# Hedgehog linear attention and a maxout FFN on one core: transposes by the crossbar, 64-row paired projections, strips of nine tiles, and an order written by hand

## The chip, the cores and the metric

The kernel runs on one core of a Trainium2 chip. A core has five engines that each work through an instruction queue of their own: TensorE (PE in the profile, with its weight loads shown apart as PEld), VectorE (DVE), ScalarE (ACT), GpSimd (POOL) and SyncE (SP), which here only issues transfers. Sixteen DMA engines move data. PE writes only to the accumulator memory PSUM, which has eight banks of 512 fp32 values in each of 128 partitions. The metric is the device time of one execution in microseconds (us), lower is better.

## The reference

```python
q, k, v: (8, 8, 576, 64) fp32          # batch, heads, tokens, head width
w_phi: (64, 128)   moe_w1, w2, w3: (512, 768)   moe_w_out: (768, 512)

def phi(x):                            # 64 -> 256 features
    proj = x @ w_phi                                        # (..., 576, 128)
    proj = proj - max(abs(proj), axis=-1, keepdims=True)
    return concatenate([exp(proj), exp(-proj)], axis=-1)
q_p, k_p = phi(q), phi(k)
kv  = einsum('bhsf,bhsd->bhfd', k_p, v)
z   = sum(k_p, axis=2)
num = einsum('bhsf,bhfd->bhsd', q_p, kv)
den = einsum('bhsf,bhf->bhs', q_p, z)[..., None] + 1e-6
x   = (num / den), heads side by side  # (4608, 512)
h   = maximum(maximum(x @ w1, x @ w2), x @ w3)
out = h @ w_out                        # (4608, 512) fp32
```

## The kernel before

**Units.** The 64 pairs of batch and head are taken four at a time: 16 units of four heads, 2,304 rows of q, k and v each, so two units make one batch of 576 tokens. A unit's rows lie in 18 tiles of 128 rows (two heads of 576 rows fill nine tiles, half a tile each: partitions 0 to 63 hold the first head, 64 to 127 the second). That block of two heads is called a strip.

**Loads.** `loads` brings q, k and v of a unit as fp32 by three queues (q by SP L214, k by ACT L216, v by POOL L218), one unit ahead, into double buffers. `prepare` then has DVE cast q and k side by side into `qk_bf` (L226, L227) and v into `v_bf` (L228). PE transposes the 18 tiles of `qk_bf` (L234, `tps`) and DVE copies them from PSUM to `qkT` (L235), with q's 64 rows in partitions 0 to 63 and k's in 64 to 127.

**Groups.** `group` takes four tiles (five groups a unit, the last of two tiles). Per tile a 64-row matmul gives the projection of q (`psq`, L265) and one that of k (`psk`, L267), rows on the partitions. DVE takes both maxima (L269 `mq_bf`, L271 `mk_f`), ACT makes exp of plus and minus the keys' projection (L273, L274). Then the same q projection is computed a second time with the features on the partitions (`psTt`, L278, one matmul of 512 columns on 128 rows, half of them zero weights), q's maxima are subtracted from it by one matmul per tile (L281, weights `mq_bf` spread over 128 columns, times minus the identity), and ACT makes both exponentials `Eq1T`, `Eq2T` (L298, L299). The keys' maxima are not subtracted; `emit_va_vb` scales v with exp of them instead (ACT L252, L253, POOL L254, L256).

**Two units later** (`LAG`): `kv_strip` sums keys times values over the nine tiles of a strip by 64-row matmuls of 65 columns (`kvps`, L316), `xt_nums` multiplies with the queries' features (`psnd`, L333, L335), DVE divides (`rden`, `x_sb`, L338 to L343), and `xt_trans` transposes the result on PE (`pxT`, L356) and copies it to `xT_all` on DVE (L360).

**FFN.** Chunks of up to 512 tokens are cut into items: for each of six blocks of 128 hidden features twelve matmuls of 512 columns (`ups`, L137), one copy on ACT and two maxima on DVE (L147 to L152); then per 128 tokens six matmuls (`ops`, L161), a copy on ACT (L169) and a store by POOL's queue (L112). `ffn_filler` puts one item behind a group or a transposed head.

**PSUM.** One pool, `psA`, with eight buffers of one bank serves every tile that PE writes. The order of each engine's instructions comes from a scheduler that goes by the order of the code and by which buffers are free.

Of the kernel before, what the change touches and what calls it, by code (L numbers as in the profile page):

```python
# [12 lines left out]
LN = mybir.ActivationFunctionType.Ln  # L14
ALU = mybir.AluOpType
# [4 lines left out]
NTOK = B * S  # L20
# [3 lines left out]

UNITS = 16
UROWS = 2304
HU = 4
UT = UROWS // P
GROUPS = [(0, 4), (4, 4), (8, 4), (12, 4), (16, 2)]
HALVES = [(0, 5), (5, 4)]  # L30
LAG = 2
# [3 lines left out]
def kernel(  # L35
    ctx: ExitStack,
    tc: tile.TileContext,
    q: bass.AP,
    k: bass.AP,
    v: bass.AP,  # L40
    w_phi: bass.AP,
    moe_w1: bass.AP,
    moe_w2: bass.AP,
    moe_w3: bass.AP,
    moe_w_out: bass.AP,
    out: bass.AP,
):
    nc = tc.nc

    try:  # L50
        from concourse.hw_specs import get_activation_tables
        _tables = list(get_activation_tables(nc.m.arch).keys())
        _set_id = _tables.index("natural_log_exp_and_others")
    except Exception:
        _set_id = 6
    nc.scalar.add_instruction(
        mybir.InstLoadActFuncSet(
            act_func_set_id=_set_id,
            name=nc.get_next_instruction_name(),
            ins=[],  # L60
            outs=[],
# [3 lines left out]
    q_flat = q.rearrange("b h s d -> (b h s) d")  # L65
    k_flat = k.rearrange("b h s d -> (b h s) d")
    v_flat = v.rearrange("b h s d -> (b h s) d")

    const = ctx.enter_context(tc.tile_pool(name="const", bufs=1))
# [3 lines left out]
    negident = const.tile([P, P], BF16, name="negident")  # L73
    nc.gpsimd.tensor_single_scalar(negident, ident, -1.0, ALU.mult)
    wphi2 = const.tile([P, DF], BF16, name="wphi2")
    wphi_q = const.tile([P, DF], BF16, name="wphi_q")
    nc.gpsimd.memset(wphi_q[D:2 * D, :], 0.0)
    wphi_f = const.tile([P, DF], FP32, name="wphi_f")
    nc.sync.dma_start(wphi_f[0:D, :], w_phi)
    nc.sync.dma_start(wphi_f[D:2 * D, :], w_phi)  # L80
    nc.vector.tensor_copy(wphi2, wphi_f)
    nc.vector.tensor_copy(wphi_q[0:D, :], wphi_f[0:D, :])

    w_bf = [const.tile([P, DM // P, DFF], BF16, name=f"w{wi}_bf") for wi in range(3)]
    wout_bf = const.tile([P, DFF // P, DM], BF16, name="wout_bf")

    def load_weights():
        for wi, w_ap in enumerate((moe_w1, moe_w2, moe_w3)):
            nc.gpsimd.dma_start(w_bf[wi], w_ap.rearrange("(ct p) n -> p ct n", p=P))
        nc.gpsimd.dma_start(wout_bf, moe_w_out.rearrange("(ct p) n -> p ct n", p=P))  # L90

    raw = ctx.enter_context(tc.tile_pool(name="raw", bufs=2))
    vpool = ctx.enter_context(tc.tile_pool(name="vpool", bufs=2))
    qkp = ctx.enter_context(tc.tile_pool(name="qkp", bufs=2))
    epool = ctx.enter_context(tc.tile_pool(name="epool", bufs=3))
    mpool = ctx.enter_context(tc.tile_pool(name="mpool", bufs=2))
    kvpool = ctx.enter_context(tc.tile_pool(name="kvpool", bufs=3))
    denp = ctx.enter_context(tc.tile_pool(name="denp", bufs=2))
    ffp = ctx.enter_context(tc.tile_pool(name="ffp", bufs=2))
    psA = ctx.enter_context(tc.tile_pool(name="psA", bufs=8, space=bass.MemoryType.PSUM))  # L100

    xT_all = const.tile([P, DM // P, NTOK], BF16, name="xT_all")

    ffn_items = deque()
    ffn_pending = deque()
    out_dma_pending = deque()
    ffn_count = [0]

    def flush_out_dmas(keep: int = 0):
        while len(out_dma_pending) > keep:  # L110
            dram_ap, osb = out_dma_pending.popleft()
            nc.gpsimd.dma_start(dram_ap, osb)  # L112

    def flush_pending_ffn():
        while ffn_pending:
            ffn_items.append(ffn_pending.popleft())
            ffn_count[0] += len(ffn_items[-1])

    def pop_ffn_item():
        while ffn_items and not ffn_items[0]:  # L120
            ffn_items.popleft()
        if not ffn_items:
            return None
        item = ffn_items[0].popleft()
        ffn_count[0] -= 1
        return item

    def make_ffn_items(tok0: int, ntok: int):
        hT = ffp.tile([P, DFF // P, 512], BF16, name="hT", tag="hT")
        chunk_items = deque()  # L130

        for j in range(DFF // P):
            def item(j=j, hT=hT):
                def umat(i):
                    up = psA.tile([P, 512], FP32, name="ups", tag="b")
                    for ct in range(DM // P):
                        nc.tensor.matmul(  # L137
                            up[:, 0:ntok],
                            lhsT=w_bf[i][:, ct, j * P:(j + 1) * P],
                            rhs=xT_all[:, ct, tok0:tok0 + ntok],  # L140
                            start=(ct == 0),
                            stop=(ct == DM // P - 1),
                        )
                    return up
                u1 = umat(0)
                t1 = ffp.tile([P, 512], BF16, name="t1", tag="t1")
                nc.scalar.copy(t1[:, 0:ntok], u1[:, 0:ntok])  # L147
                u2 = umat(1)
                t2 = ffp.tile([P, 512], BF16, name="t2", tag="t2")
                nc.vector.tensor_tensor(t2[:, 0:ntok], t1[:, 0:ntok], u2[:, 0:ntok], ALU.max)  # L150
                u3 = umat(2)
                nc.vector.tensor_tensor(hT[:, j, 0:ntok], t2[:, 0:ntok], u3[:, 0:ntok], ALU.max)  # L152
            chunk_items.append(item)

        ntt = (ntok + P - 1) // P
        for tt in range(ntt):
            def item(tt=tt, hT=hT):
                mrow = min(P, ntok - tt * P)
                ops_ = psA.tile([P, DM], FP32, name="ops", tag="b")
                for j in range(DFF // P):  # L160
                    nc.tensor.matmul(  # L161
                        ops_[0:mrow, :],
                        lhsT=hT[:, j, tt * P:tt * P + mrow],
                        rhs=wout_bf[:, j, :],
                        start=(j == 0),
                        stop=(j == DFF // P - 1),
                    )
                osb = ffp.tile([P, DM], FP32, name="osb", tag="osb")
                nc.scalar.copy(osb[0:mrow, :], ops_[0:mrow, :])  # L169
                out_dma_pending.append((out[tok0 + tt * P:tok0 + tt * P + mrow, :], osb[0:mrow, :]))  # L170
            chunk_items.append(item)
        ffn_pending.append(chunk_items)

    def ffn_filler(n=1):
        for _ in range(n):
            item = pop_ffn_item()
            if item is None:
                return
            flush_out_dmas(keep=2)
            item()  # L180

    chunks = []
    tok = 0
    last_batch_start = (B - 1) * S
    while tok < NTOK:
        n = min(512, NTOK - tok)
        if tok < last_batch_start < tok + n:
            n = last_batch_start - tok
        chunks.append((tok, n))
        tok += n  # L190
    next_chunk = [0]

    def ffn_ready(tokens_done: int, final: bool = False):
        while next_chunk[0] < len(chunks):
            tok0, ntok = chunks[next_chunk[0]]
            if tok0 + ntok <= tokens_done:
                make_ffn_items(tok0, ntok)
                next_chunk[0] += 1
            else:
                break  # L200

    class Unit:
        def __init__(un, u):
            un.u = u
            un.b = u // 2
            un.hbase = (u % 2) * HU
            un.row0 = u * UROWS

        def loads(un):
            un.q_raw = raw.tile([P, UT, D], FP32, name="q_raw", tag="q_raw")  # L210
            un.k_raw = raw.tile([P, UT, D], FP32, name="k_raw", tag="k_raw")
            un.v_raw = raw.tile([P, UT, D], FP32, name="v_raw", tag="v_raw")
            r0 = un.row0
            nc.sync.dma_start(un.q_raw.rearrange("p (st j) d -> p st j d", st=2),  # L214
                              q_flat[r0:r0 + UROWS, :].rearrange("(st p j) d -> p st j d", st=2, p=P))
            nc.scalar.dma_start(un.k_raw.rearrange("p (st j) d -> p st j d", st=2),  # L216
                                k_flat[r0:r0 + UROWS, :].rearrange("(st p j) d -> p st j d", st=2, p=P))
# [41 lines left out]
        def group(un, gi):  # L259
# [43 lines left out]
            elif t0 + gsz == UT:  # L303
                un.emit_va_vb(9, UT)
# [147 lines left out]
```

## Time and profile before

| | |
|---|---|
| time, median of three runs | 447.31 us (445.69 to 449.65) |
| span of the profiled execution | 445.3 us |
| granted TensorE clock, mean | 0.951 |
| PE busy | 398.1 us (89%), 4,286 matmuls |
| DVE busy | 324.9 us (73%), 762 instructions |
| ACT busy | 207.8 us (47%), 514 |
| POOL busy | 116.7 us (26%), 145 |
| DMA moved | 41.62 MB, mean 93 GB/s |

The span runs from the first to the last instruction of the profiled execution; no other time of that execution was taken, and it lies 2.0 us below the median of the runs. Busy time of an engine is the union of its instructions' times; a matmul's time includes the run through the array, so that neighbours overlap, and how fast PE really works is read from the starts of one run of matmuls and the next. Instructions are named by tile and by line of the kernel.

### The profile page before, as it was taken

Reading aid. Unit: us, or ns where it says so; the run is one execution under the profiler, and the core shown is the slowest. Engines: PE = TensorE matmul, PEld = TensorE weight load, DVE = VectorE, ACT = ScalarE, POOL = GpSimd, SP = SyncE. Lnnn points to the kernel's source line nnn. Section 1 sums busy time; section 2 is a strip of 40 time slices with the busy share of each in tenths; the row PEclk is TensorE's granted clock in tenths of the full one; section 3 lists DMA queues with packets and bytes.
Section 4 is the critical chain, followed back from the end, with each engine's and each line's share of the span. In section 5 each row is a group of like instructions: output and inputs, shape, how many; then the busy total and the mean of one; then the engine's idle time right before and its main releaser. Section 6 shows DMA issues by size and latency. Waiting matters only on the chain.

```text
span 445.3 us, 10421 instructions
## 1 busy us (share of the span) xinstructions
PE 398.1 (89%) x4286; PEld 227.8 (51%) x4286; DVE 324.9 (73%) x762; ACT 207.8 (47%) x514; POOL 116.7 (26%) x145
## 2 busy tenths in 40 slices
PE   0599888998999899998999899989999989899993
PEld 0367566446564456455654556445644555444442
DVE  0697999975888689967897698868977876724331
ACT  1096746451754546562736275454656461132322
POOL 3156145023150504023422315050402240010101
PEclk9996796997999989998999899998999999999998
DMA  8999142512324033312531232001000100020202
GB/s 297 327 244 259 68 160 89 179 54 79 125 67 148 25 110 124 115 45 79 177 110 54 76 126 77 31 25 49 27 0 1 72 25 2 1 96 11 72 36 71
DMA packets 16479, 41.62 MB, mean 93 GB/s; under 512 B 1456, under 2 KB 3888, under 8 KB 16432
## 3 DMA queue, kind: packets, MB, share of 16 engines
q0 software_dynamic: 7568, 22.02, 16.9%
q10 hardware_dynamic: 4352, 9.44, 6.4%
q1 hardware_dynamic: 4512, 9.50, 6.3%
q8 instruction: 33, 0.54, 0.5%
q14 instruction: 14, 0.11, 0.1%
HBM read 34.67 MB, written 9.44 MB: 99 GB/s over the span
## 4 chain that ended last, share of the span: by engine, by line
PE 56%; issue 18%; ACT 9%; DVE 8%; DMA 4%; POOL 3%; SPq 0%; POOLq 0%; ACTq 0%
PE ups L137 22%; PE ops L161 7%; PE pxT L356 6%; PE psnd L333 4%; PE psq L265 4%; PE psTt L278 4%; PE tps L234 4%; PE psTt L281 3%; DMA q_raw<-in_q_dram 3%; ACT Eq1T L298 2%; ACT Eq2T L299 2%; PE psnd L335 2%; DVE mq_bf L269 2%; POOL va L254 2%; DVE qk_bf L227 2%
## 5 line engine op out<-in xcount | busy, mean ns | idle before, releaser
L137 PE MATMUL ups<-xT_all,w_bf 128*128 128x512 bf16 (+2 forms) x720 | 152.0, 358 | 0.1
L298 ACT ACTIVATE Eq1T<-psTt 128x512 bf16<-128x512 f32 (+1 forms) x96 | 51.5, 541 | 127.4 <-PE psTt L281 107.5
L137 PEld LDWEIGHTS <-w_bf 128*128 128x128 bf16 x720 | 62.3, 98 | 62.3 <-issue 0.6
L256 POOL TENSOR_TENSOR vb<-v_bf,em 128x585 bf16<-128x585 bf16 x32 | 37.6, 1176 | 147.2 <-ACT emn L253 86.7
L112 POOL DMA_DIRECT2D out_dram<-osb x37 | 22.7, 613 | 136.0 <-ACT osb L169 116.3
L161 PE MATMUL ops<-wout_bf,hT 128*128 128x512 bf16 (+1 forms) x222 | 56.1, 383 | 0.0
L299 ACT ACTIVATE Eq2T<-psTt 128x512 bf16<-128x512 f32 (+1 forms) x96 | 52.8, 551 | 0.0
L360 DVE COPY xT_all<-pxT 64x576 bf16<-64x576 bf16 x64 | 47.8, 746 | 6.2 <-PE pxT L356 5.5
L269 DVE TENSOR_REDUCE mq_bf<-psq 128x4 bf16<-128x512 f32 (+1 forms) x80 | 50.4, 630 | 2.5 <-PE psk L267 2.1
L271 DVE TENSOR_REDUCE mk_f<-psk 128x4 f32<-128x512 f32 (+1 forms) x80 | 50.1, 626 | 0.1
L333 PE MATMUL psnd<-kv_sb,Eq1T 128*128 128x65 bf16 (+1 forms) x320 | 38.3, 208 | 12.8 <-DVE kv_sb L322 11.3
L254 POOL TENSOR_TENSOR va<-v_bf,emn 128x585 bf16<-128x585 bf16 x32 | 38.5, 1204 | 5.6 <-ACT emn L253 5.6
L335 PE MATMUL psnd<-kv_sb,Eq2T 128*128 128x65 bf16 (+1 forms) x320 | 38.2, 205 | 0.0
L356 PE MATMUL pxT<-ident,x_sb 128*64 128x128 bf16 (+1 forms) x320 | 35.8, 225 | 2.4 <-DVE x_sb L341 2.3
L356 PEld LDWEIGHTS <-x_sb 128*64 128x64 bf16 (+1 forms) x320 | 23.0, 109 | 27.8 <-issue 17.9
L234 PE MATMUL tps<-ident,qk_bf 128*128 128x128 bf16 x288 | 26.1, 264 | 12.3 <-DVE qk_bf L227 12.3
L281 PE MATMUL psTt<-negident,mq_bf 128*128 128x128 bf16 x288 | 31.7, 232 | 5.0 <-DVE mq_bf L269 4.9
L265 PE MATMUL psq<-wphi_66,qkT 64*128 64x128 bf16 x288 | 32.7, 234 | 3.7 <-DVE qkT L235 3.7
L333 PEld LDWEIGHTS <-Eq1T 128*128 128x128 bf16 (+1 forms) x320 | 26.5, 105 | 17.8 <-DVE kv_sb L322 10.8
L267 PE MATMUL psk<-wphi_66,qkT 64*128 64x128 bf16 x288 | 32.3, 233 | 1.5 <-DVE xT_all L360 1.1
L278 PE MATMUL psTt<-qkT,wphi_q 128*128 128x512 bf16 (+1 forms) x80 | 32.0, 400 | 1.2 <-ACT Ek_969 L274 0.4
L281 PEld LDWEIGHTS <-mq_bf 128*128 128x128 bf16 x288 | 20.1, 102 | 22.8 <-DVE mq_bf L269 13.5
(309 smaller groups left out, 587.5 us busy)
## 6 DMA issues: line engine op xcount, KB each, us to landing
k_raw<-in_k_dram ACTq DMA_DIRECT2D x16, 576.0 KB, 4.7
v_raw<-in_v_dram POOLq DMA_DIRECT2D x16, 576.0 KB, 5.6
q_raw<-in_q_dram SPq DMA_DIRECT2D x16, 576.0 KB, 5.4
out_dram<-osb POOLq DMA_DIRECT2D x35, 256.0 KB, 2.5
w_bf<-in_moe_w_dram POOLq DMA_DIRECT2D x3, 768.0 KB, 12.4
wout_bf<-in_moe_w_out_dram POOLq DMA_DIRECT2D x1, 768.0 KB, 7.6
out_dram<-osb POOLq DMA_DIRECT2D x2, 128.0 KB, 2.3
wphi_f<-in_w_phi_dram SPq DMA_DIRECT2D x2, 32.0 KB, 4.9
```

The lines of the kernel that those rows point to most:

```text
L137: nc.tensor.matmul(up[:, 0:ntok], lhsT=w_bf[i][:, ct, j * P:(j + 1) * P], rhs=xT_all[:, ct, tok0:tok0 + ntok], start=(ct == 0), stop=(ct = ...
L161: nc.tensor.matmul(ops_[0:mrow, :], lhsT=hT[:, j, tt * P:tt * P + mrow], rhs=wout_bf[:, j, :], start=(j == 0), stop=(j == DFF // P - 1),)
L265: nc.tensor.matmul(psq[:, i, :], lhsT=un.qkT[0:D, cols], rhs=wphi2[0:D, :], start=True, stop=True)
L269: nc.vector.tensor_reduce(un.mq_bf[:, t0:t0 + gsz], psq[:, 0:gsz, :], AXX, ALU.max, apply_absolute_value=True)
L271: nc.vector.tensor_reduce(un.mk_f[:, t0:t0 + gsz], psk[:, 0:gsz, :], AXX, ALU.max, apply_absolute_value=True)
L278: nc.tensor.matmul(psTt[:, 0:ncols], lhsT=wphi_q, rhs=un.qkT[:, t0 * P:t0 * P + ncols], start=True, stop=False)
L281: nc.tensor.matmul(psTt[:, i * P:(i + 1) * P], lhsT=un.mq_bf[:, t0 + i:t0 + i + 1].to_broadcast([P, P]), rhs=negident, start=False, stop=( ...
L298: nc.scalar.activation(eq_view(un.Eq1T), src, EXP)
L299: nc.scalar.activation(eq_view(un.Eq2T), src, EXP, scale=-1.0)
L333: nc.tensor.matmul(psnd[0:ncolc, c, :], lhsT=un.Eq1T[:, col0:col0 + ncolc], rhs=kv_sb[:, 0, :], start=True, stop=False)
L356: nc.tensor.transpose(pxT[0:D, 128 * c:128 * c + ncolc], x_sb[0:ncolc, c, :], ident[0:ncolc, 0:ncolc])
L360: nc.vector.tensor_copy(dstv, srcv)
```

## The change

The kernel is written anew around the same mathematics; units, strips and the lag stay, and all of the following changes.

- **Loads and transposes.** POOL's queue loads k and q and casts them to bf16 on the way (`kn`, `qn`); SP's queue loads v as fp32. SP then issues two crossbar transposes per unit (`kT`, `qT`, 128x1152 each) in place of PE's 18 and DVE's copies. Loads are issued two units ahead with three buffers (four for v).
- **Projections.** A transposed block of 128 partitions holds two tiles, one in partitions 0 to 63, one in 64 to 127, so that two 64-row matmuls with weights `wphi` in both halves run as a pair, for k, for q, and for the second, transposed projection of q (`psT`). Steps are of three blocks, six tiles: three steps a unit, 48 in all.
- **q's maxima.** DVE writes them to a zeroed 128x128 tile `mq`, SP transposes it on the crossbar to `mT`, and six matmuls with constant weights `pick` subtract them two steps later.
- **Result.** `num_strip` treats both heads of a strip in one PSUM tile of two banks, DVE writes x of a batch to `x_main` (four groups of 128 tokens) and `x_rest` (the last 64), and SP transposes these on the crossbar (`xT`, `xrest`). The last ninth of the tokens of four batches is one FFN chunk of 256 tokens; every batch has one chunk of 512.
- **PSUM.** Two pools: `ps2`, two buffers of two banks, for `psk`, `psq`, `psT` and `nd` in turn; `ps1`, four buffers of one bank, for `kvps`, `ups` and `ops`.
- **Order.** The scheduler is off; the order is that of the code. `fill` puts FFN pieces (four or six matmuls each) at three places of a step, and `pace` spreads a batch's pieces over six steps, less a reserve of 5.0. Stores go by SP's queue.

```diff
+    ps2 = ctx.enter_context(tc.tile_pool(name="ps2", bufs=2, space=bass.MemoryType.PSUM))
+    ps1 = ctx.enter_context(tc.tile_pool(name="ps1", bufs=4, space=bass.MemoryType.PSUM))
+    ctx.enter_context(tc.manual_schedule())
...
+    def start_loads(u):
...
+        load(nc.gpsimd, un.kn, k_f, u)
+        load(nc.gpsimd, un.qn, q_f, u)
+        load(nc.sync, un.vn, v_f, u)
...
+    def transposes(un):
...
+        nc.sync.dma_start_transpose(un.kT, un.kn.rearrange("p s d -> p (s d)"))
+        nc.sync.dma_start_transpose(un.qT, un.qn.rearrange("p s d -> p (s d)"))
...
+    def project(dst, xT, b0):
+        for i in range(GB):
+            for e in range(2):
+                nc.tensor.matmul(dst[:, e, i * P:(i + 1) * P], lhsT=xT[e * D:(e + 1) * D, b0 + i, :],
+                                 rhs=wphi[e * D:(e + 1) * D, :], start=True, stop=True)
...
+    def queries(un, g):
...
+        nc.vector.tensor_reduce(mq[:, :, 0:GB], view(pq), AXX, ALU.max, apply_absolute_value=True)
+        mT = small.tile([P, P], BF16, name="mT", tag="mT", bufs=4)
+        nc.sync.dma_start_transpose(mT, mq.rearrange("p e d -> p (e d)"))
...
+    def transposed(un, g):
...
+        for e in range(2):
+            rows = slice(e * D, (e + 1) * D)
+            nc.tensor.matmul(pv[:, e], lhsT=wphi[rows, :],
+                             rhs=un.qT[rows, b0:b0 + GB, :].rearrange("d b (h p) -> d h b p", h=2),
+                             start=True, stop=False)
+        for i in range(GB):
+            for e in range(2):
+                rows = slice(e * D, (e + 1) * D)
+                nc.tensor.matmul(pv[:, e, :, i, :], lhsT=pick[rows, i, :],
+                                 rhs=mT[rows, :].rearrange("r (h p) -> r h p", h=2),
+                                 start=False, stop=(i == GB - 1))
+        for s in range(2):
+            nc.scalar.activation(un.Eq[s][:, :, :, b0 * D:(b0 + GB) * D],
+                                 pt[:, :, 0:GB * P].rearrange("f e (h n) -> f e h n", h=2),
+                                 EXP, scale=1.0 - 2.0 * s)
...
+    def finish_batch(b):
...
+        nc.sync.dma_start_transpose(xT, x_main.rearrange("p c n -> p (c n)"))
+        nc.sync.dma_start_transpose(xrest[:, :, b, :], x_rest)
...
+    for n in range(STEPS + 4):
+        u, g = divmod(n, NG)
...
+        us = pace(n)
+        tt = n - LAG_T
+        if 0 <= tt < STEPS:
+            transposed(units[tt // NG], tt % NG)
+        if n < STEPS:
+            pk = keys(units[u], g)
+        fill(us / 3)
+        if n < STEPS:
+            for s in range(2):
+                keys_exp(units[u], g, pk, s)
+            queries(units[u], g)
+            if g == 1 and u + 1 < UNITS:
+                transposes(units[u + 1])
+            if g == 2 and u + 2 < UNITS:
+                units[u + 2] = start_loads(u + 2)
+            if g >= 1:
+                scale_v(units[u], g - 1)
+        t = n - 3
+        if t >= 0:
+            r = t % NG
+            if r < 2 and t < STEPS:
+                kvs[t // NG, r] = kv_strip(units[t // NG], r)
+        fill(us / 3)
+        t = n - 4
+        if t >= 0 and t % NG < 2:
+            r = t % NG
+            num_strip(units[t // NG], r, kvs.pop((t // NG, r)))
+        fill(us / 3)
+        if t >= 0 and t % NG == 1:
+            done = units.pop(t // NG)
+            if done.half == 1:
+                enqueue(finish_batch(done.b))
+                if done.b % 4 == 3:
+                    enqueue(rest_chunk(done.b - 3))
+    fill(1e9)
```

What the change moves is seen best on three queues. First PE in the middle of the program, where a unit begins. Before, behind the last `psnd` of an older unit, with runs of equal rows cut to the first and the weight loads left out:

```order
L335 MATMUL psnd<-kv_sb,Eq2T 64x65
L234 MATMUL tps<-ident,qk_bf 128x128
L265 MATMUL psq<-wphi_66,qkT 128x128
L267 MATMUL psk<-wphi_66,qkT 128x128
L278 MATMUL psTt<-qkT,wphi_q 128x512
L356 MATMUL pxT<-ident,x_sb 64x128
L137 MATMUL ups<-xT_all,w_bf 128x512
L281 MATMUL psTt<-negident,mq_bf 128x128
```

And one step of the changed kernel on PE, with the engines that a row waits for:

```order
L189 MATMUL psT<-qT,wphi 128x384 [waits Activation_49]
L195 MATMUL psT<-mT,pick 128x2x64 [waits DMAHW5_49]
L152 MATMUL psk<-wphi,kT 128x128 [waits PE_49]
L289 MATMUL ups<-xT,w_bf 128x512
L152 MATMUL psq<-wphi,qT 128x128 [waits Activation_49]
L222 MATMUL kvps<-va_1432,Ek_1427 128x65 [waits Pool_49]
```

The transposes `tps` and `pxT` are gone, a piece of the FFN stands between the keys' and the queries' projections, and `psq` now waits for ACT, because its PSUM buffer is the one that the step's `psT` leaves. Second, SP's queue. Before, it only loads q, each load when DVE has read the buffer:

```order
L79 DMA wphi_f<-in_w_phi_dram 64x128
L214 DMA q_raw<-in_q_dram 128x2x576 x2
L214 DMA q_raw<-in_q_dram 128x2x576 [waits DMAHW2_49,DVE_49]
L214 DMA q_raw<-in_q_dram 128x2x576 [waits DMAHW4_49,DMAHW0_49,DVE_49]
L214 DMA q_raw<-in_q_dram 128x2x576 [waits DMAHW6_49,DVE_49]
```

In the changed kernel, around the end of one batch:

```order
L106 DMA_TRANSPOSE kT<-kn 128x9x128 [waits DMASW6_49]
L107 DMA_TRANSPOSE qT<-qn 128x9x128 [waits DMAHW3_49,DMASW7_49]
L179 DMA_TRANSPOSE mT<-mq_105 128x128 [waits DMAHW4_49,DVE_49]
L83 DMA vn<-in_v_dram 128x2x576 [waits DMAHW5_49,Pool_49]
L329 DMA out_dram<-osb 2x64x512 [waits DMAHW6_49,Activation_49]
L323 DMA_TRANSPOSE xT<-x_main 128x16x128 [waits DMAHW7_49,DVE_49]
L324 DMA_TRANSPOSE xrest<-x_rest 128x4x64 [waits DMAHW0_49,DVE_49]
L329 DMA out_dram<-osb 2x64x512 [waits DMAHW1_49,Activation_49]
L179 DMA_TRANSPOSE mT<-mq_106 128x128 [waits DMAHW2_49,DVE_49]
```

SP had 18 transfers and now has 152, and all crossbar transposes, loads of v and stores stand in one line; each waits for its data and for the transfer eight places ahead of it (DMAHW0 to DMAHW7 are the semaphores that they share in turn). Third, DVE over one step of the changed kernel:

```order
L165 TENSOR_REDUCE mk<-psk 128x2x3
L296 TENSOR_TENSOR t_1353<-t_1327,ups 128x512
L177 TENSOR_REDUCE mq_105<-psq 128x2x3
L299 TENSOR_TENSOR hT<-t_1353,ups 128x512
L250 RECIPROCAL rd<-nd 128x8
L251 RECIPROCAL rr<-nd 64x2
L252 TENSOR_TENSOR x_main<-nd,rd 128x2x4x64
L254 TENSOR_TENSOR x_rest<-nd,rr 64x128
```

Casts of the inputs, copies of `qkT` and copies to `xT_all` are gone from DVE; what is left are the reductions, now 48 of each kind over six tiles, the FFN's maxima, `kv_sb` and the division for two heads at once.

More of the change, by code (lines that the diff above doesn't have):

```diff
@@ L23, with hedgehog_ffn @@
 P = 128
[L25 to L26 removed]
 HU = 4
[L28 to L31, printed above, removed]
[L34 to L47 removed]
+UNITS = B * H // HU
+UROWS = HU * S
+NT = 18
+NB = 9
+NG = 3
+GB = 3
+J = 9
+TOK = (0, 1, 4, 5, 8)
+CT = DM // P
+FT = DFF // P
+D1 = D + 1
+STEPS = UNITS * NG
+LAG_T = 2
+RESERVE = 5.0
+@with_exitstack
+def hedgehog_ffn(ctx, tc, q, k, v, w_phi, moe_w1, moe_w2, moe_w3, moe_w_out, out):
     nc = tc.nc
@@ L71 @@
+    wphi = const.tile([P, DF], BF16, name="wphi")
+    nc.vector.tensor_copy(wphi, wphi_f)
+    NQ = 4
+    mqs = [const.tile([P, 2, D], BF16, name=f"mq{i}") for i in range(NQ)]
+    for t in mqs:
+        nc.gpsimd.memset(t, 0.0)
     ident = const.tile([P, P], BF16, name="ident")
     make_identity(nc, ident)
[L73 to L90, printed above, removed]
@@ L100 @@
[L100 to L148, printed above, removed]
-                t2 = ffp.tile([P, 512], BF16, name="t2", tag="t2")
[L150 to L172, printed above, removed]
@@ new lines, in kv_strip @@
+    def kv_strip(un, r):
+        kv = [ps1.tile([P, 2, D1], FP32, name="kvps", tag="b") for _ in range(2)]
+        for s in range(2):
+            Ek = tiles(un.Ek[s])
+            for j in range(J):
+                for h in range(2):
+                    rows = slice(h * D, (h + 1) * D)
+                    nc.tensor.matmul(kv[h][:, s, :], lhsT=Ek[rows, r * J + j, :],
+                                     rhs=un.va[s][rows, r * J + j, :], start=(j == 0), stop=(j == J - 1))
+        kv_sb = small.tile([P, 2, 2, D1], BF16, name="kv_sb", tag="kv_sb", bufs=4)
+        for h in range(2):
+            nc.vector.tensor_copy(kv_sb[:, h], kv[h])
+        return kv_sb
```

432 lines of the change are left out of this document (179 added, 253 removed).

## The prediction

> **What bounds the kernel now.** I read the page's busy times first, then its slices and its chain.
>
> ```profile
> PE 398.1 (89%) x4286; PEld 227.8 (51%) x4286; DVE 324.9 (73%) x762; ACT 207.8 (47%) x514; POOL 116.7 (26%) x145
> PE   0599888998999899998999899989999989899993
> PE 56%; issue 18%; ACT 9%; DVE 8%; DMA 4%; POOL 3%; SPq 0%; POOLq 0%; ACTq 0%
> ```
>
> PE is busy for 398.1 of 445.3 us, and the chain that ends last runs mostly on it; DVE is a good second. Since a matmul's record includes its run through the array, I ask next how many stretches PE is really full in.
>
> ```profile
> 10.00:40.00 30.00, 22.21 (x256) 15.05 (x256) 23.51 (x47) 18.16 (x50) 11.96 (x13) 0.94 1.06 263
> 220.00:250.00 30.00, 28.98 (x307) 15.62 (x306) 23.06 (x51) 15.85 (x41) 8.95 (x10) 1.00 0.25 80
> 400.00:430.00 30.00, 30.00 (x145) 13.91 (x143) 13.22 (x20) 7.87 (x14) 2.16 (x4) 1.00 0.09 31
> ```
>
> Columns are the stretch, its length, busy time of PE, PEld, DVE, ACT and POOL, granted clock, DMA share, GB/s. Before there is FFN work (10 to 40) PE has gaps of a quarter; in the middle it is full, and from 400 on it does FFN alone. So PE's own work sets the middle and the end, and I price PE by the starts of successive runs in the timeline, at clock 1.00:
>
> ```profile
> 211.24 0.23 PE L265 MATMUL psq<-wphi_66,qkT 64*128 64x128 bf16 x1
> 211.31 0.22 PE L265 MATMUL psq<-wphi_66,qkT 64*128 64x128 bf16 x1
> ...
> 211.57 0.39 PE L278 MATMUL psTt<-qkT,wphi_q 128*128 128x512 bf16 x1
> 211.89 0.55 PE L356 MATMUL pxT<-ident,x_sb 128*64 128x128 bf16 x5
> ...
> 217.65 0.77 PE L316 MATMUL kvps<-va,Ek_2993 64*128 64x65 bf16 x15
> ...
> 219.21 0.48 PE L316 MATMUL kvps<-vb,Ek_2994 64*128 64x65 bf16 x18
> ...
> 220.51 0.20 PE L333 MATMUL psnd<-kv_sb,Eq1T 128*128 128x65 bf16 x1
> ...
> 221.04 0.20 PE L333 MATMUL psnd<-kv_sb,Eq1T 128*128 128x65 bf16 x1
> ...
> 222.11 1.18 PE L234 MATMUL tps<-ident,qk_bf 128*128 128x128 bf16 x18
> ...
> 224.17 0.55 PE L356 MATMUL pxT<-ident,x_sb 128*64 128x128 bf16 x5
> 224.66 0.82 PE L137 MATMUL ups<-xT_all,w_bf 128*128 128x512 bf16 x3
> 225.31 0.39 PE L281 MATMUL psTt<-negident,mq_bf 128*128 128x128 bf16 x4
> 225.54 2.10 PE L137 MATMUL ups<-xT_all,w_bf 128*128 128x512 bf16 x9
> 227.57 0.55 PE L356 MATMUL pxT<-ident,x_sb 128*64 128x128 bf16 x5
> ```
>
> From these: a group's four q,k pairs with the change of mode take 0.33 us (211.24 to 211.57), one 512-column `psTt` 0.32, four maxima 0.23 (225.31 to 225.54), one head's `pxT` 0.49 (224.17 to 224.66), one head's `psnd` 0.53 (220.51 to 221.04), a unit's `kvps` 2.0 (217.65 to 219.69), its `tps` 1.18, and a 512-column FFN matmul 0.226 (nine from 225.54 to 227.57).
>
> **PE before and after.** A unit has 4.5 groups' worth of tiles. Before: 1.18 + 4.5 x (0.33 + 0.32 + 0.23) + 2.0 + 4 x 0.53 + 4 x 0.49 = 11.2 us. The FFN has 720 `ups` and 222 `ops` over 4,608 tokens, together 864 matmuls' worth of 512 columns: 864 x 0.226 = 195 us. Sixteen units and the FFN make 375; the other 23 of the 398.1 are half-clock stretches like the 0.94 above, and wider gaps.
>
> After: `tps` and `pxT` go. A step has three `psk` pairs and three `psq` pairs of 128 columns at 0.055 each (the spacing between 211.24 and 211.57, less the change of mode, about 0.1 each way), `psT` as one pair of 384 columns (0.17) and three pairs of 128 for the maxima (0.165). With two visits to the 64-row mode a step (0.2 each): 0.165 + 0.165 + 0.17 + 0.165 + 0.4 = 1.06. The 384-column pair is the paired form of what ran on 128 rows with half the weights zero; it halves these columns. `kvps` and `nd` keep their counts, 36 and 20 matmuls a strip. A unit: 3 x 1.06 + 2.0 + 2.12 = 7.3 us. **Saved on PE: 3.9 x 16 = 62 us**, and PE's work is 16 x 7.3 + 195 = 312.
>
> **DVE and ACT** have to stay below that, else the saving stops at them.
>
> ```profile
> L360 DVE COPY xT_all<-pxT 64x576 bf16<-64x576 bf16 x64 | 47.8, 746 | 6.2 <-PE pxT L356 5.5
> L235 DVE COPY qkT<-tps 128x1024 bf16<-128x1024 bf16 (+1 forms) x48 | 24.4, 552 | 6.3 <-PE tps L234 5.3
> L227 DVE CAST qk_bf<-k_raw 128x1152 bf16<-128x1152 f32 x16 | 14.0, 876 | 0.0
> L269 DVE TENSOR_REDUCE mq_bf<-psq 128x4 bf16<-128x512 f32 x64 | 43.7, 683 | 2.4 <-PE psk L267 2.1
> L269 DVE TENSOR_REDUCE mq_bf<-psq 128x2 bf16<-128x256 f32 x16 | 6.7, 416 | 0.1
> L341 DVE TENSOR_TENSOR x_sb<-psnd,rden 128x256 bf16<-128x256 f32 x64 | 26.1, 407 | 5.8 <-PE pxT L356 5.7
> L152 DVE TENSOR_TENSOR hT<-t_1361,ups 128x512 bf16<-128x512 bf16 x1 | 0.7, 689 | 0.0
> ```
>
> These three kinds of copies and casts alone are 86 us that leave DVE. A reduction costs (683 - 416) / 256 = 1.04 ns per element, so one over 768 takes 0.95 us; two per step, 1.9. The FFN's maxima, 12 per batch chunk at 0.69 in six steps, add 1.4, the casts and the division (0.67 for 512 elements by L341's row, and some 0.6 beside it) about 1.2 on average: 4.5 us a step.
>
> ```profile
> 208.39 0.39 PE L281 MATMUL psTt<-negident,mq_bf 128*128 128x128 bf16 x4
> ...
> 208.81 0.60 ACT L298 ACTIVATE Eq1T<-psTt 128x512 bf16<-128x512 f32 x1 [8.72 <-PE psTt L281]
> 209.31 0.59 ACT L299 ACTIVATE Eq2T<-psTt 128x512 bf16<-128x512 f32 x1
> ...
> 220.71 0.47 ACT L273 ACTIVATE Ek_3464<-psk 128x256 bf16<-128x256 f32 x1
> 220.98 0.49 ACT L274 ACTIVATE Ek_3465<-psk 128x256 bf16<-128x256 f32 x1
> ```
>
> ACT's exponentials start 0.50 us apart at 512 elements and 0.27 at 256, so 0.73 at 768: four a step are 2.9, with the copies for the FFN (about 1.1) and exp for v (0.4) 4.4 us. Both are under PE's step below, but not by much.
>
> **A step in the middle.** FFN pieces are put at steps 9 to 50. The last chunks (21.7 + 10.8 us for 512 and 256 tokens) and the reserve (5.2) are left for the end, so 195 - 38 = 157 us go into 42 steps: 3.75 each, in three pieces of 1.25. PE's step is 7.3 / 3 + 3.75 = 6.2 us. Then a wait that the change adds: `psq` takes the PSUM buffer that `psT` held, so it waits for both `Eq` exponentials. `psT` ends 0.6 after the step begins, ACT starts 0.03 later (208.39 + 0.39 to 208.81), two exponentials end at 0.65 + 0.73 + 0.87 = 2.25; PE is ready at 0.7 + 1.25 = 1.95. PE, with all behind `psq` in its queue, waits 0.3, with the signal 0.35. The next buffers come in time: `nd` needs the keys' exponentials, ended at about 3.8, and PE is there at 3.8 to 4.9; the next `psk` needs DVE's last division 1.4 us after `nd`, and PE has 1.25 + 0.45 of work until then. **A step is 6.55, 42 of them 275 us.**
>
> **Start and end.**
>
> ```profile
> 12.29 2.10 PE L234 MATMUL tps<-ident,qk_bf 128*128 128x128 bf16 x18 [12.29 <-DVE qk_bf L227]
> L137 PE MATMUL ups<-xT_all,w_bf x720: 189/379/390, 78.7 to 436.8; 128*128 128x512 bf16 x144, 128*128 128x448 bf16 x18, 128*128 128x64 bf16 x18
> 439.28 0.54 POOL L112 DMA_DIRECT2D out_dram<-osb  x1 [2.71 <-ACT osb L169]
> v_raw<-in_v_dram POOLq DMA_DIRECT2D x16, 576.0 KB, 5.6
> ```
>
> PE starts at 12.3 now: loads, two casts. After, a load with cast (5.6 us, longer beside others) and two transposes in a row: 13. Steps 0 to 8 have no FFN to fill them and are a chain through the two buffers: `psT`, two exponentials, `psk`, reduction, two exponentials, `nd`, division; by the durations above 4 us while the pipeline fills and 5.0 to 5.2 after, 42 for nine, and 3 for weights (3 MB) and loads that share the queues. FFN starts at 13 + 45 = 58 us, where it is 78.7 now. Behind step 50: 38 us of FFN, 4 of waiting for the last `xT` beyond the reserve, and 7 from the last matmul (438.4) to the end of the span. **58 + 275 + 49 = 382 us**, and the median of the runs lies 2 above the span: 384.
>
> **The crossbar** is the unknown; no row shows one of its transfers. Per unit and DMA engine it moves, if in pieces of 128 elements, (1152 + 1152 + 384 + 1152) / 16 = 240 pieces of 256 bytes (`kT`, `qT`, three `mT`, half of `xT` and `xrest`).
>
> ```profile
> q0 software_dynamic: 7568, 22.02, 16.9%
> q10 hardware_dynamic: 4352, 9.44, 6.4%
> q1 hardware_dynamic: 4512, 9.50, 6.3%
> q1 hardware_dynamic: 42, 0.02, 4.5%
> ```
>
> The first three rows are the whole run, the last a window of 1.4 us (2.6 to 4.0) with w_phi's 512-byte packets: 0.045 x 16 x 1.4 us / 42 = 24 ns each. A packet of q10 takes 0.064 x 16 x 445.3 / 4352 = 105 ns for 2.2 KB. Between 24 and 105 I take 24, the row nearest in size: 5.8 us per unit, beside about 8.2 of other transfers (29.6% of the span on the three queues) and a unit of 19.7 us: hidden. `kT` and `qT` are issued two steps (13 us) ahead, `mT` one and a half; 72 pieces at 24 ns and some 2 to 5 us of landing fit. SP's issue time per transpose is in no row; from 0 to 4 us a large one would still fit (152 issues in 315 us).
>
> The Trainium skill has two prices that disagree. "VectorE: DVE Perf Modes", section "The three transpose paths", gives 1309 ns for one 128x128 by the crossbar; 31 blocks a unit one after another would be 41 us, 650 in all. "DMA: Bandwidth & Descriptors", section "Latency and other measured facts", gives 261 GB/s for transposes, an estimated 4 us a unit, hidden. By the packet rows the trace leans to the second (128 packets of 512 bytes at 24 ns, eight per engine, are 0.2 us of an engine); no run here shows either yet.
>
> **Rivals.** (1) The crossbar binds and the kernel is **slower**. At 105 ns a piece an engine has 25.2 + 8.2 = 33.4 us per unit, 16 of them 534 us. Above (19.7 - 8.2) / 240 = 48 ns transfers set the pace, above 77 ns (445 - 20 over 16 units) the result is slower than before. For it: small pieces in other rows cost more per byte, and all transposes stand in one queue. Against: 24 ns at 512 bytes. (2) ACT and DVE, at 4.4 and 4.5 of 6.55 us and strictly in order, fall behind: one FFN copy (0.5) ahead of the keys' exponentials and one maximum (0.69) ahead of the division delay `nd` and the next `psk`, some 0.85 a step: 382 + 36 = 418, 420 as a time. For it: only two buffers where eight were, so that each wait reaches PE. (3) The waits vanish: 382 - 15 (0.35 x 42) - 9 at start and end = 358, 360 as a time. (4) It does not do what it says: loads or weights come late enough that PE's 62 us turn into waits, no change, 447.
>
> **How the numbers follow.** The forecast (365 to 400) gets 0.48, (2) 0.22, (3) 0.12, (1) 0.14, (4) 0.04. The range takes in the forecast, (2) and (3), with (2) up to 435, a price of 1.2 us a step, and (3) down to 345 for faster FFN matmuls (the last stretch above has 145 in 30.0 us, 0.207 each with some narrow ones; 864 x 0.019 = 16 us): 0.82. About 1% is what a measurement of this kernel tells from no change; faster 0.82, same 0.04, slower 0.14.
>
> **What would show it.** `ups` should start near 58 us; PE's busy time should fall to 310 to 335 and its `psq` wait for ACT by 0.3 us in most steps; DVE should be near 225 us busy, ACT near 210; transposes of 128x1152 should land within 8 us, and DMA's share should stay below 0.8 in the middle. I am wrong if PE waits for `kT`, `qT` or `mT` (rival 1), if `nd` and `psk` wait for DVE and ACT by more than half a microsecond a step (2), or if the early steps take over 7 us each.

## The result, and the profile after

The changed kernel takes **496.23 us** (median, 494.77 to 499.29) beside 447.04 for the kernel before, measured along with it: a ratio of 1.1104 [1.1034, 1.1174], 11% slower. Forecast were 384 us and a range of 345 to 435. The time came out on the other side of the kernel before, the side of rival 1. Ratios, here and below, are of the fast executions alone, those within 1.5% of a kernel's fastest, while medians are of all.

The page of the changed kernel: span, busy times, slices of PE, clock and DMA, the two large queues, the chain.

```profile
span 493.8 us, 8999 instructions
PE 337.6 (68%) x3688; PEld 182.2 (37%) x3688; DVE 213.8 (43%) x409; ACT 199.3 (40%) x353; POOL 111.2 (23%) x176
PE   0146256888549967696868936999547967977990
PEclk9999976999797988799786978999797988897996
DMA  8979973839873999449583879839884261042012
q1 hardware_dynamic: 73664, 34.62, 46.5%
q0 software_dynamic: 11072, 12.59, 20.4%
DMA 40%; PE 35%; ACT 10%; issue 5%; DVE 3%; SPq 3%; POOL 1%; ACTq 0%; POOLq 0%
```

The compute engines shed about what the sum said: PE is at 337.6 us busy where 398.1 stood, DVE at 213.8 where 324.9 stood. But PE was 89% busy and is now 68%, and the chain that ends last, 4% DMA before, is 40% DMA. The waits of PE (us in all, times, longest) name the transfers:

```profile
PE psT L195 <- DMA mT<-mq: 38.1, 11, 5.9
PE ups L289 <- DMA xT<-x_main: 38.1, 8, 6.5
PE psk L152 <- DMA kT<-kn: 36.8, 7, 21.0
PE psq L152 <- ACT Eq L199: 15.5, 24, 1.3
```

The three longest waits are for crossbar transposes. It looks like rival 1 at first sight: the row of q1 gives 0.465 x 16 x 493.8 / 73664 = 50 ns a packet. The rows of one stall say otherwise. First two transposes of the chain from 180 us on, then the DMA engines over the same stretch (tenths of their busy time, 40 slices of 0.575 us), then the stores and two of the transposes that SP issues:

```profile
179.53 0.51 SPq L329
180.14 10.16 DMA mT<-mq
...
194.24 8.77 DMA kT<-kn
```

```profile
DMA  0201114999120015899951113119911111111899
out_dram<-osb SPq DMA_DIRECT2D x3, 256.0 KB
```

```profile
183.64 10.51 SPq L179 DMA_TRANSPOSE mT<-mq  x1
194.24 4.64 SPq L106 DMA_TRANSPOSE kT<-kn  x1
```

L329 is a store of 128 rows of output. Behind it, one `mT` of 32 KB takes 10.16 us, and `kT` 8.77. The DMA engines are not full while this happens: 24 of the 40 slices stand at 2 tenths or less, although `kn` and `qn` of a later unit load in the same stretch. The last stores have the engines to themselves (the answer on DMA for 450 to 464 us; slices of 0.35 us):

```profile
DMA  1101111113111111111111111111111111111111
DMA packets 339, 0.70 MB, mean 50 GB/s; under 512 B 4, under 2 KB 4, under 8 KB 338
q1 hardware_dynamic: 338, 0.68, 13.1%
```

Of the 338 packets 4 are tiny and 334 have 2048 bytes. They take 14 us and 13.1% of 16 engines, steadily 1 tenth in 38 of 40 slices: **a store runs on 2.1 of the 16 DMA engines**, and its 128 packets take 5.4 us. The reading that follows: the pieces of a transpose that belong to these two engines wait until it is through, and the others are soon done and idle. Here the Trainium skill has a rule that I passed over: "DMA: Bandwidth & Descriptors", section "Rules for kernel authors", says that the number of engines follows from the slowest dimension of the access patterns, and that an outermost dimension below 16 confines the transfer to that many. The store's rows in DRAM, `rows[TOK[c]:TOK[c]+3:2]`, have an outermost dimension of 2. The rows above agree.

### The profile page after: what moved, and what is told of

Same layout as the page of the kernel before. It is cut to its first block, busy times and chain, and to the rows that moved or that the text cites. A ratio compares the mean times of both kernels' runs of the same rounds, so it can differ in the third digit from the quotient of the medians.

```text
span 493.8 us, 8999 instructions
## 1 busy us (share of the span) xinstructions
PE 337.6 (68%) x3688; PEld 182.2 (37%) x3688; DVE 213.8 (43%) x409; ACT 199.3 (40%) x353; POOL 111.2 (23%) x176
## 3 DMA queue, kind: packets, MB, share of 16 engines
q1 hardware_dynamic: 73664, 34.62, 46.5%
## 4 chain that ended last, share of the span: by engine, by line
DMA 40%; PE 35%; ACT 10%; issue 5%; DVE 3%; SPq 3%; POOL 1%; ACTq 0%; POOLq 0%
PE ups L289 20%; DMA kT<-kn 12%; DMA mT<-mq 10%; DMA xT<-x_main 10%; ACT Eq L199 8%; DMA qT<-qn 5%; PE ops L304 4%; PE nd L238 4%; DMA kn<-in_k_dram 3%; PE kvps L222 3%; DVE mq L177 3%; PE psq L152 2%; ACT osb L307 1%; PE psT L195 1%; PE psT L189 1%
## 5 line engine op out<-in xcount | busy, mean ns | idle before, releaser
L289 PE MATMUL ups<-xT,w_bf 128*128 128x512 bf16 x576 | 157.8, 418 | 38.1 <-DMA xT<-x_main 38.1
L209 POOL TENSOR_TENSOR va<-vn,em 128x576 bf16<-128x576 f32 x64 | 73.6, 1150 | 305.0 <-ACT em L207 286.7
L199 ACT ACTIVATE Eq<-psT 128x768 bf16<-128x768 f32 x96 | 72.7, 811 | 84.4 <-PE psT L195 84.3
L165 DVE TENSOR_REDUCE mk<-psk 128x6 f32<-128x768 f32 x48 | 46.0, 958 | 109.6 <-PE psk L152 109.6
L170 ACT ACTIVATE Ek<-psk 128x768 bf16<-128x768 f32 x96 | 73.2, 825 | 33.7 <-DVE mk L165 33.5
L296 DVE TENSOR_TENSOR t<-t,ups 128x512 bf16<-128x512 bf16 (+1 forms) x60 | 38.0, 633 | 60.3 <-PE ups L289 52.8
L177 DVE TENSOR_REDUCE mq<-psq 128x6 bf16<-128x768 f32 x48 | 46.0, 959 | 28.8 <-PE psq L152 28.1
L304 PE MATMUL ops<-wout_bf,hT 128*128 128x512 bf16 x216 | 52.6, 386 | 0.0
L195 PE MATMUL psT<-mT,pick 64*128 64x128 bf16 x288 | 18.8, 243 | 38.2 <-DMA mT<-mq 38.1
L238 PE MATMUL nd<-kv_sb,Eq 128*128 128x65 bf16 (+1 forms) x640 | 40.5, 209 | 3.0 <-DVE mq L177 2.1
L299 DVE TENSOR_TENSOR hT<-t,ups 128x512 bf16<-128x512 bf16 (+1 forms) x60 | 37.8, 631 | 10.0 <-PE ups L289 6.8
```

Source lines behind the costliest of these rows:

```text
L165: nc.vector.tensor_reduce(un.mk[:, b0:b0 + GB, :].rearrange("p b e -> p e b"), view(pk), AXX, ALU.max, apply_absolute_value=True)
L170: nc.scalar.activation(slots(un.Ek[s], g * GB), view(pk), EXP, scale=1.0 - 2.0 * s)
L177: nc.vector.tensor_reduce(mq[:, :, 0:GB], view(pq), AXX, ALU.max, apply_absolute_value=True)
L199: nc.scalar.activation(un.Eq[s][:, :, :, b0 * D:(b0 + GB) * D], pt[:, :, 0:GB * P].rearrange("f e (h n) -> f e h n", h=2), EXP, scale=1.0 ...
L209: nc.gpsimd.tensor_tensor(un.va[s][:, t, 0:D], un.vn[:, t, :], em.to_broadcast([P, J, D]), ALU.mult)
L238: nc.tensor.matmul(nd[0:n * D, h, c * D1:(c + 1) * D1], lhsT=un.Eq[s][:, e, h, b * D:(b + n) * D], rhs=kv_sb[:, h, s, :], start=(s == 0), ...
```

## The experiments

Theory S: the stores on two engines hold up the transposes. Rivals: X, the crossbar's own rate (rival 1 of the prediction), and Q, SP's queue is too long or in a bad order. Ratios are to the kernel before, on the same chip.

**Split stores.**

```
-            nc.sync.dma_start(rows[TOK[c]:TOK[c] + 3:2], osb)
+            for h in range(2):
+                nc.sync.dma_start(rows[TOK[c] + 2 * h], osb[h * D:(h + 1) * D, :])
```

> The changed kernel, each 256 KB store of output issued as two stores of 64 rows; nothing else differs. Theory S (stores): a whole store, 128 packets of 2048 B at about 84 ns, goes through two of the 16 DMA engines and takes 5.5 us there; every crossbar transpose needs all 16 engines and waits behind it, while the transposes' own pieces take 18 ns (median). Split, a store spreads over the engines: then the waits of PE for kT, qT, mT and xT (some 115 us with the weight loads' waits) mostly go and the time is 385 to 415. Theory X (the crossbar's own rate): the pieces, 41 ns in the mean, are slow by themselves; 480 to 500, no change. Theory Q (SP's queue is too long, too many issues in order): 32 issues more, 495 to 510.

Measured 390.27 us (387.43 to 396.74), ratio **0.8702 [0.8635, 0.8769]**: S, and X and Q miss by 90 us and more. The profile is of the longest of the four executions (396.74 us). The page, the DMA answer for 203 to 205 us (195 store packets, and 48 tiny ones), and the waits:

```profile
span 395.0 us, 9015 instructions
PE 314.4 (80%) x3672; PEld 175.0 (44%) x3688; DVE 212.8 (54%) x409; ACT 198.7 (50%) x353; POOL 111.3 (28%) x176
PE 50%; DMA 25%; ACT 11%; issue 5%; DVE 3%; SPq 3%; POOL 1%; ACTq 0%; POOLq 0%
```

```profile
DMA packets 243, 0.40 MB, mean 200 GB/s; under 512 B 48, under 2 KB 48, under 8 KB 243
q1 hardware_dynamic: 243, 0.40, 93.4%
```

```profile
PE psk L152 <- DMA kT<-kn: 27.2, 5, 19.2
PE psq L152 <- ACT Eq L199: 15.1, 24, 1.3
PE ups L289 <- DMA xT<-x_main: 11.1, 4, 5.5
PE psT L195 <- DMA mT<-mq: 6.2, 4, 2.0
```

The same bytes now move at 200 GB/s where 50 were, on 15 engines: 195 store packets in 2 us, 1.3 us for 128. The packet records of the transposes agree: their 61,440 pieces of 256 bytes take 18 ns each in the median of both kernels, but 41 ns in the mean with whole stores, the longest 8.6 us, and 26 with split ones, the longest 1.7. The waits for `mT`, `xT` and `kT` fall from 113 to 45 us, 19 of these for the first unit's `kT`.

Where the 99 us between the two profiled executions lie follows from the `ups` matmuls of the changed kernel and of this one:

```profile
L289 PE MATMUL ups<-xT,w_bf x576: 376/379/634, 78.1 to 464.9; 128*128 128x512 bf16 x192
L289 PE MATMUL ups<-xrest,w_bf x144: 272/273/421, 277.2 to 478.1; 128*128 128x256 bf16 x144
```

```profile
L289 PE MATMUL ups<-xT,w_bf x576: 376/379/634, 75.0 to 373.9; 128*128 128x512 bf16 x192
L289 PE MATMUL ups<-xrest,w_bf x144: 272/273/283, 232.0 to 387.0; 128*128 128x256 bf16 x144
```

3 us are lost before the FFN starts (78.1 and 75.0), 8 behind the last `ups` (15.7 us to the end of the span and 8.0; the last stores stand there), and 88 from the first to the last `ups` (400 and 312). Over nearly that stretch the windows give PE's share, the clock and the DMA engines, first the changed kernel, then the split stores:

```profile
78.00:465.00 387.00, 296.07 (x3178) 153.47 (x3178) 182.81 (x352) 165.97 (x294) 81.82 (x126) 0.88 0.66 87
```

```profile
75.00:374.00 299.00, 272.71 (x3164) 145.83 (x3178) 182.09 (x352) 165.28 (x294) 81.91 (x126) 0.98 0.64 113
```

Of 88 us more, 65 are PE's idle time (90.9 and 26.3) and 23 the same matmuls at a lower granted clock (0.88 and 0.98). The DMA share is 0.66 in one and 0.64 in the other: the mean over 16 engines does not show which of them a transfer waits for.

**Whole stores from ScalarE's queue.**

```
-            nc.sync.dma_start(rows[TOK[c]:TOK[c] + 3:2], osb)
+            nc.scalar.dma_start(rows[TOK[c]:TOK[c] + 3:2], osb)
```

> The changed kernel, whole stores as they are (two DMA engines each), but issued from ScalarE's queue instead of SP's. S: the two engines are as busy as before; if they take turns between the queues, a piece waits for one packet (18 + 84 ns) until the store is through, so a transpose still ends when the store does or up to 5 us sooner: 440 to 490. Q (order in SP's queue alone): the transposes are free of the stores, 385 to 415. X: 480 to 500.

Measured 479.84 us, ratio 1.0691 [1.0606, 1.0776], inside the range of S, and just below that of X, which the split stores had ruled out. Out of the transposes' queue, but in the same form, the stores still cost 89 of 107 us; the order in SP's queue alone is not the cause. PE's waits move: those for `mT` and `xT` shrink to 1.9 and 14.1 us, those for `kT` and `qT` grow. A new cost comes in as well, since ScalarE itself stands in the issue of a store for up to 6.2 us. How much of the 89 is ScalarE's was not separated.

```profile
PE psk L152 <- DMA kT<-kn: 41.1, 6, 21.8
PE psq L152 <- DMA qT<-qn: 30.6, 8, 9.1
L329 ACTq DMA_DIRECT2D out_dram<-osb x32: 521/528/6199, 114.7 to 453.5; - x32
```

**The kernel before with strided stores.** The stores of the kernel before go to SP's queue and take the form with an outermost dimension of 2, which puts the rows of each 128 in another order in the output.

```
-            nc.gpsimd.dma_start(dram_ap, osb)
+            if osb.shape[0] == P:
+                nc.sync.dma_start(dram_ap.rearrange("(p j) n -> j p n", j=2), osb)
+            else:
+                nc.sync.dma_start(dram_ap, osb)
```

> The kernel before, its stores put on SP's queue and in the strided form (row order of each 128 rows permuted in the output: two groups of 64 rows), so that each uses two DMA engines for 5.5 us; there are no crossbar transposes. S says that the loss needs both, transposes that are waited for and stores on two engines: 445 to 455, with 3 to 5 us more at the end, and the loads of q, issued a unit ahead, stretched but hidden. If such stores cost by themselves: 35 of them by 3 us, 500 or more.

Measured 508.22 us, ratio 1.137 [1.1302, 1.1438]: the range under S failed, and the other one, 500 or more, held. There is no transpose to hold up, and the kernel still loses 61 us. The waits show a different way to the same loss, ScalarE waiting for an `osb` tile that a store still reads:

```profile
ACT osb L172 <- DMA out_dram<-osb: 55.8, 12, 6.8
```

**The same with four `osb` tiles** (`bufs=4` on `osb`).

> The kernel before with the strided stores on SP's queue (output rows permuted), and four osb tiles instead of two. If its loss of 61 us was ACT's wait for an osb tile that a store on two DMA engines still reads (55.8 us in that run), it mostly goes: 450 to 465. If the loads of q behind the stores are the cause: 490 to 510.

Measured 454.11 us, ratio 1.0145 [1.0101, 1.0188]. So 55 of the 61 us were that buffer; with four tiles, as the changed kernel has, stores on two engines, and their move to SP's queue, which was not tried alone, cost 1.5%. S needs a wider wording: a store on two engines costs where somebody waits behind it, a transpose or a buffer.

**`kT` and `qT` transposed twice**, with split stores.

```
+        for t, n in ((un.kn, "k2T"), (un.qn, "q2T")):
+            again = trans.tile([P, NB, P], BF16, name=n, tag=n)
+            nc.sync.dma_start_transpose(again, t.rearrange("p s d -> p (s d)"))
```

> As the split stores, and the transposes of kT and qT are issued a second time into tiles that nothing reads: 144 pieces more per DMA engine and unit. X with 41 ns a piece: 5.9 us more per unit on DMA engines that set the pace, 60 to 95 us above the split stores alone. S with 18 ns: 2.6 us per unit on engines that are about half busy, plus 32 issues on SP: 0 to 12 us above the split stores alone.

Measured 435.79 us, ratio 0.9749 [0.9679, 0.9819]: 47 us above the split stores by the ratios, which neither expectation had. The chain, two rows of it near the start, and PE's waits:

```profile
PE 41%; DMA 26%; SPq 16%; ACT 10%; DVE 4%; issue 2%; ACTq 0%; DVEq 0%; POOLq 0%
34.28 9.71 SPq L110
44.09 11.47 DMA mT<-mq
```

```profile
PE ups L292 <- DMA xT<-x_main: 30.8, 7, 9.9
PE psT L198 <- DMA mT<-mq: 27.5, 8, 18.0
```

SP stands 9.71 us in the issue of a second copy (L110), and the next `mT`, which PE wants within a step or two, is issued and served only behind it. Over the whole run PE's waits for `mT` and `xT` rise from 17 to 58 us. Whether order or the engines' time costs this is told by two more runs.

**Maxima on PE**, with split stores: the 48 transposes of maxima go, and six products a step with a negative identity take their place.

```
...
-                nc.tensor.matmul(pv[:, e, :, i, :], lhsT=pick[rows, i, :],
-                                 rhs=mT[rows, :].rearrange("r (h p) -> r h p", h=2),
+                nc.tensor.matmul(pv[:, e, :, i, :], lhsT=mq[:, e, i:i + 1].to_broadcast([P, P]),
+                                 rhs=negident.rearrange("r (h p) -> r h p", h=2),
...
```

> Split stores, and the maxima are subtracted as in the kernel before (six 128x128 products a step of the maxima with a negative identity), so that the 48 crossbar transposes of the maxima go. PE gets 3 x 0.055 us more per step, 8 us in all. If the waits behind these transposes matter (PE waited 6.2 us for mT, and kT and qT stand behind them on SP's queue): 376 to 386. If they were hidden: 394 to 400.

Measured 388.89 us, ratio 0.8677 [0.8642, 0.8712]: level with the split stores, between the two expectations. PE is busy 324.7 us, 10 more, and the waits that went make up for it.

**Maxima on PE, `kT` and `qT` twice.**

> Split stores, maxima on PE, and kT and qT transposed a second time into tiles that nothing reads. The doubling cost 45.5 us where mT, the maxima's transposes, stood behind them. If it was the order (what is waited for soon stands behind what is not): much of it goes, 392 to 405. If it was the DMA engines' time, 2.6 us a unit one for one: 428 to 436.

Measured 396.07 us, ratio 0.8856 [0.8786, 0.8926]: by the ratios the doubling now costs 8 us where it cost 47, inside the range for the order. So 39 of the 47 go when no small transposes, wanted soon, stand behind the large ones; the added pieces themselves cost 8 us at most.

**`kT` and `qT` a step earlier**, with split stores: issued at `g == 0` instead of `g == 1`.

> Split stores, and kT and qT of the next unit are transposed in a unit's first step instead of its second (three steps ahead instead of two). In the split-store run PE still waited 27.2 us for kT (19.2 of it for the first unit, which stays) and 5.5 for qT. If these transposes are late because they are issued late (latency), some 13 us go: 374 to 380. If the DMA engines or SP's queue are full (throughput), or the maxima's transposes now stand behind them instead, nothing goes: 386 to 395.

Measured 400.24 us, ratio 0.8874 [0.8833, 0.8916]: by the ratios some 8 us slower than the split stores, above both expectations. The profile is of the longest execution (403.94 us). PE waits less for `kT` (20.6 us, all of it the first unit's), and more for the maxima, 23.1 us where 6.2 stood:

```profile
PE psT L195 <- DMA mT<-mq: 23.1, 6, 9.1
```

**Weights three steps later**, with split stores: `load_weight` at steps 4 to 7 instead of 1 to 4.

> Split stores, and the four weight loads are issued at steps 4 to 7 instead of 1 to 4. In the split-store run the FFN started at 75.0 us where 58 was forecast, and the loads of unit 1 took 11 us beside the weights. If the 3 MB of weights stretch the first loads and transposes: FFN starts near 62 and the time is 376 to 384. If the early steps are slow for another reason (order on SP, the chain through PSUM): within 2 us of the split stores, about 390.

Measured 386.48 us, ratio 0.8652 [0.8613, 0.8692], between the two expectations; the interval overlaps with that of the split stores. The FFN starts at 71.1 us, not at 62: the weights are a small part of the late start.

**Both together**, maxima on PE and later weights.

> Split stores, maxima on PE, weight loads three steps later. If what each gave alone adds up (1.4 and 3.8 us off 390.3): 384 to 387. If they share a cause (the first units' queue) and the early waits of PE for kT go altogether: 376 to 383.

Measured 385.14 us, ratio 0.862 [0.8563, 0.8677], as the parts add up; the FFN starts at 67.6 us. This is the lowest median of all, 14% below the kernel before; the split of the stores alone gives 13 of the 14, and the two intervals overlap.

**Both, and `kT`, `qT` a step earlier.**

> As the one before, and kT and qT transposed in a unit's first step. This cost 10 us where the maxima's transposes stood behind them on SP's queue. If that was the reason: without these transposes it now costs nothing, 376 to 387, level with the run before it or up to 8 us faster. If earlier transposes cost by themselves (they meet the loads): 392 to 398.

Measured 386.92 us, ratio 0.8632 [0.8552, 0.8712]: level. With no maxima in the queue, the earlier transposes cost nothing, and gain nothing.

**Whole stores, maxima on PE.**

> The changed kernel with its whole stores, but the maxima on PE. In the changed kernel PE waited 38 us for mT, 38 for xT and 37 for kT. If the stores hurt only through what stands right behind them and is wanted at once (mT): 385 to 410. If every transpose behind a store on two DMA engines stalls: the waits for kT and xT stay or take over, 440 to 475.

Measured 487.66 us, ratio 1.0944 [1.0883, 1.1004], above both expectations. Without the transposes of maxima nearly the whole loss stays, 101 us beside the same kernel with split stores:

```profile
PE psk L154 <- DMA kT<-kn: 59.2, 7, 23.1
PE ups L288 <- DMA xT<-x_main: 37.3, 8, 6.5
```

Transposes behind a whole store stall, `kT` too, which is issued two steps ahead.

## Why the prediction was wrong

**The step that failed** is the term of the other transfers in the part on the crossbar, "beside about 8.2 of other transfers (29.6% of the span on the three queues)", with the "hidden" that rests on it. The term is a mean over 16 engines, taken from the kernel before, whose stores were contiguous rows. The change gives the stores a new row order; I counted their issues on SP's queue and not the engines that their form runs on. In its place the runs showed 32 stores of 5.4 us on two engines, some 170 us in which the pieces of a transpose that fall to these two wait. What it costs is the difference to the split stores: 1.1104 - 0.8702 of 447, 107 us. "Hidden" was thus wrong, though not by the crossbar's price.

**Rival 1** named the right side and two of the three large waits, `kT` and `mT`, by the wrong mechanism; it named `qT`, which was waited for 3.7 us, and not `xT`, with 38.1. A stretch of the split-store kernel with transposed pieces alone (232 to 234.5 us) gives their price:

```profile
DMA packets 1811, 0.46 MB, mean 182 GB/s; under 512 B 1811, under 2 KB 1811, under 8 KB 1811
```

16 engines x 2.5 us / 1811 is 22 ns a piece, where I had taken 24 between 24 and 105. Of the two prices of the Trainium skill this stands nearer to the 261 GB/s of "DMA: Bandwidth & Descriptors", section "Latency and other measured facts" (there for a middle dimension that is not contiguous), than to the 1309 ns for a 128x128 of "VectorE: DVE Perf Modes", section "The three transpose paths", which would be an estimated 25 GB/s.

**What held**, judged on the split-store kernel. PE's busy time 314.4 (310 to 335 foreseen), DVE 212.8 (near 225), ACT 198.7 (near 210). PE's wait in `psq` for the `Eq` exponentials: 15.1 us in all, where 0.35 in 42 steps were 14.7; it falls on 24 steps with 0.6 each. The rows of the middle and the end, the first from the chain, the others from PE's timeline:

```profile
75.04 3.57 PE ups L289 x8
350.63 5.34 PE L304 MATMUL ops<-wout_bf,hT 128*128 128x512 bf16 x23
358.54 15.71 PE L289 MATMUL ups<-xT,w_bf 128*128 128x512 bf16 x72 [2.57 <-DMA xT<-x_main]
```

From the first `ups` to the pieces that `pace` had held back for the end (350.63) are 275.6 us, where 275 for 42 steps were forecast. The reserve took 5.3 us (5.2), and the wait for the last `xT` 2.6 (4). Transposes land in 4.8, 6.7 and 5.8 us (`kT`, `qT`, `xT`, median) where 8 was the bound.

**What was off.** The start is 75.0, not 58; the end from the row at 358.54 to the end of the span 36.5, not 39.5 (21.7 + 10.8 for the two chunks and 7 behind the last matmul). The start's miss begins with the first transfers:

```profile
8.79 2.75 SPq L106 DMA_TRANSPOSE kT<-kn  x1
11.58 6.26 SPq L107 DMA_TRANSPOSE qT<-qn  x1
30.00:60.00 30.00, 14.15 (x258) 11.03 (x260) 12.04 (x24) 13.73 (x23) 10.49 (x16) 1.00 1.03 183
```

SP is not done issuing the first two transposes before 17.8 us (13 was my time for both to have landed), and the first `psk` runs at 19.2: 6 of the 17 us. The nine steps up to the first `ups` take 55.8 us where 45 were forecast. From 30 to 60 us the DMA engines are full (1.03) with loads, weights and transposes. Moving weights took 4 of the 17 us away, maxima on PE with it 7; the rest stays open. The start's miss cancels against the end's by 3 us only: the span of this execution is 395.0 where the sum gave 382. The median of the four, 390, lies nearer to 384 because the other executions were shorter, and of these there is no profile.

**The signs I named** were half useful. "PE waits for `kT`, `qT` or `mT`" is what happened. "DMA's share below 0.8 in the middle" held with 0.66, and was no sign of anything.

**Not settled:** that the outermost dimension alone decides the number of engines. Splitting showed that two stores of 64 rows spread and one of 2 x 64 does not; other shapes were not tried.

## What to carry to other kernels

Price a transfer by the DMA engines that it runs on, not only by its bytes: packets, duration and the share of 16 engines in a stretch where it stands alone give that number in one line. Here an `mT` of 32 KB took 10.16 us behind whole stores, and 3.2 from issue to landing in the median with split ones. So look at the shape of every other transfer, stores above all, before transposes are moved to DMA. In a queue that is served in order, what is wanted at once must not stand behind what is wanted later: doubling two transposes cost 47 us ahead of a small one and 8 without it.

## What the hardware showed that I had not expected

SP stays in the issue of a transpose much longer behind whole stores: 10.51 us for the `mT` above, with three stores just ahead of it, and 1.2 us for one with `kT` and `qT` just ahead (202.01 us in the changed kernel).

```profile
202.01 1.19 SPq L179 DMA_TRANSPOSE mT<-mq  x1
```

The stalled kernel also had the lower clock: PE's busy time for the same matmuls was 337.6 us with whole stores and 314.4 with split ones, at 0.891 and 0.982 granted. That the stalls are the reason is not shown; the kernel before, with PE 89% busy, had 0.951.
